# Sparse attention into a capacity-routed expert layer: scaling factors carried beside the rows and applied after the gather, an earlier second search, and a rearranged start

## The chip, the cores and the metric

One Trainium2 chip, one core. The metric is the time of one execution on the device in microseconds (us), the median of several runs. All times below come from the runs and the trace of the kernel before the change.

## The reference

Eight batches of eight heads, sequence 576, head dimension 64, all in fp32. Attention keeps only scores within tau of the row's largest. Its output x has 4608 rows (tokens) of 512 columns, eight blocks of 64, one for each head. A greedy router gives each token to one of eight experts with 576 places each, in order of the logits, and each expert runs a two-layer network on its own rows.

```python
scores = scale * np.matmul(q, k.transpose(0, 1, 3, 2))
thresh = np.max(scores, axis=-1, keepdims=True) - tau
attn = np.exp(masked scores - max);  attn /= attn.sum(-1) + 1e-09
x = (attn @ v) with heads side by side            # [4608, 512]
logits = x @ w_gate                               # [4608, 8]
for idx in np.argsort(-logits.flatten()):         # greedy
    tok, e = idx // 8, idx % 8
    if assigned[tok] >= 0 or counts[e] >= 576: continue
    assigned[tok] = e; counts[e] += 1
for e in range(8):
    out[assigned == e] = np.maximum(x[assigned == e] @ w1[e], 0) @ w2[e]   # 512 -> 1024 -> 512
```

## The kernel before

**Order.** The instructions of every engine stand in the order in which the Python code emits them; an engine takes its own in that order and waits by semaphores for what others make. [...] The names in the rows: PE is TensorE (its weight loads are PEld), DVE VectorE, ACT ScalarE, POOL GpSimd, SP SyncE.

**Attention** (`attention()`, to about 490 us). The 64 heads form 32 pairs; a pair has nine query tiles, so there are 288 tiles, worked two to a slot. For each tile: scores on PE (`sc`), a maximum on DVE (`z`, L74), exponentials on ACT (L85), masking on DVE (L89), transposes on PE (L98) that ACT copies out (`pt`, L113), then products with the values (`pv_unit` L144, `pl_unit` L149) into PSUM banks `xo`, copied to `xt`. The product is not yet divided by the row's denominator. `rd_calc` and `rd_unit` make the reciprocals `rd` and `rm`; `lg_unit`, `lgt_unit`, `lgm_unit` turn `xt` into logits `Lg`. For the last pair these follow each other with nothing beside them.

**Rows to memory** (`xt_unit`). One unit transposes 128 tokens of a batch back to token-major (L201) and stores them to `xrows` [4608, 512] in DRAM. The eight blocks of a row are multiplied by the eight reciprocals there. For the first two batches DVE does this as it empties the bank. The 30 units of the other six batches are put off ("late") and run beside the router's first search: ACT copies the bank (L214, 24 units) and POOL multiplies (L214 again, 128x512); six small units of 64 tokens are scaled by ACT in eight pieces (L212).

**Search** (`Router`). For each expert a threshold is searched that leaves 576 tokens. A search is `prep`, then seven steps of a DVE comparison (`cmp`), PE counting (L403), a DVE copy (`cn`), PE (L409), a DVE flag (`jka`), PE (L419 or L424) and new levels on DVE (`E`); then pick, rank and pack, which end in `idx`, the token numbers. `close` takes the chosen tokens out of the logits. Nothing else can start before the first `idx` at 536.60 us but the late units.

**Expert layer** (`moe()`). Round r works on one expert. `rows` issues five gathers by indirect DMA from POOL's queue (L615; four tiles of 128 rows and one, tile 4, of 64), transposes each tile on PE (`pt`, L625), copies it by ACT to the high part `xh` (L628), and DVE subtracts for the low part `xl`. `w1_load` and `w2_load` split the weights likewise: ACT makes `w1h` (L587) and `w2h` (L603), DVE the low parts. Layer one (L1, L645) has 192 matrix products a round (eight blocks of twelve, for two halves of the rows), from which ACT and DVE make `H`; layer two (L2, L665) has 112, five tiles in the order 0, 4, 1, 2, 3. ACT empties a tile to `y` (L668); POOL's queue stores it by an indirect DMA (L672), and POOL joins the two halves of tile 4 (L675) after tile 2. The next round's search runs inside these products, step by step, and the next round's gathers and transposes inside L2.

**The planner.** At the end of `moe()` a small loop emits the products of `ffn` one by one and advances a planned clock with each; jobs (search, loads, rows) wait in a list with planned times and are emitted when the clock passes them. `GA` is the planned time from the gathers to the first transpose, `RW` the pause behind each tile, `LATS` a pause after DVE work in the search. L1 of a round is emitted only after the planner has marked its rows done. So these numbers set where in PE's, ACT's and POOL's order a step stands, not when it runs.

Of the kernel before, what the change touches and what calls it, by code (L numbers as in the profile page):

```python
# [19 lines left out]
PPB=8; LTB=1; VTB=5; HOLD=1; CAPV=3.3; RATE=(2.4,2.4); NBO=2; XAC=(4,); NDEF=4; XTB=4; XTY=1.05; XT0=2.0; XRB=2  # L20


def attention(ctx, tc, qk, vl, tau, wgd, xrows, xts, Lg, nb_batches, ident, swap, R, after_first):
# [14 lines left out]
    def load(p):  # L38
        b,j=divmod(p,4)
        x=ld.tile([128,QK],F32,name="qk"); v=ld.tile([128,5,128],F32,name="vt",bufs=VTB)  # L40
        cut=(0,HS+S,2*(HS+S),QK) if p==0 else (0,QK)
        for n,(c,e) in enumerate(zip(cut,cut[1:])):
            nc.sync.dma_start(x[:,c:e], qk[b,j,:,c:e])
            if p==0 and n==0:
                nc.sync.dma_start(taub, bass.AP(tensor=tau.tensor,offset=tau.offset,ap=[[0,128],[1,1]]))
        if p==0: nc.sync.dma_start(wg,wgd)
        nc.sync.dma_start(v, vl[b,j])
        t={"v":v}; c=0
        for n,w in ((("k",0),HS),(("q",0),S),(("k",1),HS),(("q",1),S),(("ke",1),HS)):
            t[n]=x[:,c:c+w]; c+=w  # L50
        t["ke",0]=t["k",0]
        LD[p]=t
# [92 lines left out]
    def pl_unit(p,f):  # L145
        b,j=divmod(p,4)
        q=slice(f*HS,(f+1)*HS); xo=XO.pop((p,f))
        for h in range(2):
            T.matmul(xo[64*h:64*h+64,:HS],LD[p]["v"][:,4,64*h:64*h+64],PL[p][:,q],start=False,stop=True,skip_group_check=True)  # L149
        if f==1: have[p,"pv"]=1  # L150
        return VB[id(xo)],lambda: A.activation(XT[b][:,j,q],xo[:,:HS],AF.Copy)  # L151

# [5 lines left out]
    def rd_unit(b):  # L158
        rd=RD[b]
        ps=bank_v([128,512])  # L160
        T.matmul(ps[:,:4],swap,rd[:,:,8],start=True,stop=True)
        rm=wk.tile([128,4,2],F32,name="rm",bufs=XTB+NBO); RD["m",b]=rm
        def ev():
            V.tensor_copy(rm[0:64,:,0],rd[0:64,:,8]); V.tensor_copy(rm[64:128,:,1],rd[64:128,:,8])
            V.tensor_copy(rm[0:64,:,1],ps[0:64,:4]); V.tensor_copy(rm[64:128,:,0],ps[64:128,:4])
        return ev
    LT={}
    def lg_unit(b,f):
        if f==0: LT[b]=wk.tile([128,S+D],F32,name="lt",bufs=LTB)
        ps=bank_v([128,512])  # L170
        for j in range(4):
            T.matmul(ps[32*j:32*j+32,:HS],wg[:,j],XT[b][:,j,f*HS:(f+1)*HS],start=True,stop=True,tile_position=(0,32*j))
        def ev():
            A.activation(LT[b][:,f*HS:(f+1)*HS],ps[:,:HS],AF.Copy)
            if f==1: G.tensor_scalar(LT[b][:,S:],LT[b][:,S-D:S],1.0,0.0,op0=ALU.mult,op1=ALU.add)
        return ev
    def lgt_unit(b):
        ps=bank_v([128,4,128])
        for c in range(4): T.transpose(ps[:,c],LT[b][:,c*128:(c+1)*128],ident)
        def ev():  # L180
            w=wk.tile([128,4,2,4,8],F32,name="lw",bufs=1)
            lv=ps.rearrange("p c (j r) -> p c j r",j=4)
            for h in range(2):
                V.tensor_tensor(w[:,:,h],lv[:,:,:,8*h:8*h+8],RD[b][:,:,h:8:2].rearrange("p j c -> p c j").unsqueeze(3).to_broadcast([128,4,4,8]),op=ALU.mult)
            V.tensor_reduce(Lg[:,4*b:4*b+4,:],w.rearrange("p c h j e -> p c e (h j)"),axis=AX.X,op=ALU.add)
        return ev
    def lgm_unit(b):
        ps=bank_v([128,4,128])
        T.transpose(ps[:,0],LT[b][:,512:640],ident)
        r=slice(64*(b%2),64*(b%2)+64)  # L190
        def ev():
            w=wk.tile([128,4,2,8],F32,name="lwm",bufs=1)
            lv=ps[:,0].rearrange("p (j r) -> p j r",j=4)[:,:,:16].rearrange("p j (h e) -> p j h e",h=2)
            V.tensor_tensor(w[r],lv[r],RD["m",b][r].unsqueeze(3).to_broadcast([64,4,2,8]),op=ALU.mult)
            V.tensor_reduce(Lg[r,32+b//2,:],w[r].rearrange("p j h e -> p e (j h)"),axis=AX.X,op=ALU.add)
        return ev
    def xt_unit(b,c):
        ps=bank_v([128,4,128])
        n=128 if c<4 else 64
        for j in range(4):  # L200
            T.transpose(ps[:n,j],XT[b][:,j,c*128:c*128+n],ident)  # L201
        if b<nb_batches-NDEF-NBO: xr=wk.tile([128,512],F32,name="xr",bufs=XRB)
        else: xr=wk.tile([128,2,S],F32,name="pp",bufs=PPB)[:,0,:512]
        def ev():
            src=RD[b][:,:,2*c:2*c+2] if c<4 else RD["m",b][0:64]
            src=src.unsqueeze(3).to_broadcast([n,4,2,64])
            xv=xr[:n].rearrange("p (j h d) -> p j h d",j=4,h=2); pv=ps[:n].rearrange("p j (h d) -> p j h d",h=2)
            if b<nb_batches-NDEF-NBO: V.tensor_tensor(xv,pv,src,op=ALU.mult)
            elif c in XAC:
                for j in range(4):  # L210
                    for h in range(2):
                        A.activation(xv[:,j,h],pv[:,j,h],AF.Copy,scale=RD[b][:n,j,2*c+h:2*c+h+1] if c<4 else RD["m",b][0:64,j,h:h+1])  # L212
            else:
                A.activation(xv,pv,AF.Copy); G.tensor_tensor(xv,xv,src,op=ALU.mult)  # L214
            nc.sync.dma_start(xrows[b*S+c*128:b*S+c*128+n,:],xr[:n])
        return ev
# [6 lines left out]
    def push_pair(p):  # L223
        b,j=divmod(p,4)
        def when(n): return lambda: have.get((p,n),1<<30)+HOLD<=st["slot"]
        for f in range(2):
# [30 lines left out]
    load(0);   # L257
    if NP>1: load(1)
    after_first()
    for s_ in range(-2,NT//2+2):  # L260
# [10 lines left out]
        flush()  # L271
        for t in ev_:
# [72 lines left out]
class Router:  # L345
# [154 lines left out]
    def close(s):  # L500
        V=s.V; wk=s.wk; L=s.L

        cl=wk.tile([128,8],F32,name="cl"); V.tensor_scalar(cl,s.k("w8"),s.m,-FMAX/2,op0=ALU.is_equal,op1=ALU.mult)
        V.tensor_tensor(L,L,cl.unsqueeze(1).to_broadcast([128,NC_,8]),op=ALU.add)
        u=wk.tile([128,NC_],F32,name="u"); V.tensor_scalar(u,s.sc,BIGS,-FMAX/2,op0=ALU.is_ge,op1=ALU.mult)
        u2=wk.tile([128,NC_],F32,name="u2"); V.scalar_tensor_tensor(u2,s.sc,BIGS+CAP,u,op0=ALU.is_lt,op1=ALU.mult)
        V.tensor_tensor(L,L,u2.unsqueeze(2).to_broadcast([128,NC_,8]),op=ALU.add)
    def warm(s,n):

        ps=s.ps()  # L510
        for i in range(n): s.T.matmul(ps[:,256:384],s.ones,s.tri,start=True,stop=True)
# [26 lines left out]
    def pack(s,first):  # L538
# [4 lines left out]
        if first: s.warm(WARM[0])  # L543
        yield V.wait()
        held(0.7); s.compact(cps,poh,R)
        if first: s.warm(WARM[1])
# [6 lines left out]
LATS=[0.15,0.05,0.4]+[0.6]*5; FIX=(0.125,0.2)  # L553
GA=[7.0,5.5,7.5,9.0]; HALF=1; WARM=[20,4,50]
W1Y=5.0; L2O=(0,4,1,2,3); L2Z=1; HFB=3; RW=[0.2,0.6,1.0,2.0]; LOWP=(0,1); LPF=7; LOWT=1.4; PREPW=1; WLY=(1.0,1.0)

def moe(ctx,tc,R,start,xrows,w1,w2,out,ident):
# [10 lines left out]
    def w1_load(r,s):  # L568
        while r>0 and ("w1",r-1) not in done: yield 0.5
# [21 lines left out]
        done.add(("w1",r))  # L591
    def w2_load(r,s):
# [6 lines left out]
        while ("w1",r) not in done or (r==0 and ("x",0) not in done) or (r>0 and ("l2",r-1) not in done): yield 0.5  # L599
# [9 lines left out]
    def rows(r,s):  # L609
        while r>0 and ("x",r-1) not in done: yield 0.5  # L610
        order=(4,0,1,2,3) if r<=HALF else range(5)
        for t in order:
            n=128 if t<4 else 64
            x=wk.tile([128,D],F32,name="xg",bufs=5); s["xg",t]=x
            G.indirect_dma_start(out=x[:n],out_offset=None,in_=xrows,in_offset=IOA(ap=s["idx"][:n,t:t+1],axis=0))  # L615
        s["ei2"]=wk.tile([128,1],I32,name="ei2",bufs=2); G.tensor_copy(s["ei2"],s["ei"])
        done.add(("g",r))
        yield GA[min(r,3)]
        while r>0 and ("l1",r-1) not in done: yield 0.5
        s["xh"]=wk.tile([128,4,576],F32R,name="xh"); s["xl"]=wk.tile([128,4,576],F32R,name="xl")  # L620
        for t in order:
            n=128 if t<4 else 64
            ps=pt.tile([128,4,128],F32,name="pt")
            held[0]+=0.5
            for d in range(4): T.transpose(ps[:,d,:n],s["xg",t][:n,d*128:(d+1)*128],ident[:n,:n])  # L625
            if t<4: xv=lambda n: s[n][:,:,128*t+32*(t//2):128*t+32*(t//2)+128]; pv=ps
            else: xv=lambda n: s[n].rearrange("p k (a b) -> p k a b",a=2)[:,:,:,256:288]; pv=ps[:,:,:64].rearrange("p k (a b) -> p k a b",a=2)
            A.activation(xv("xh"),pv,AF.Copy)  # L628
            yield 0.8
            V.tensor_tensor(xv("xl"),pv,xv("xh").bitcast(F32),op=ALU.subtract)  # L630
            done.add(("row",r,t))
            if t==1: done.add(("half",r))
            yield RW[min(r,3)]
        done.add(("x",r))

    def ffn(r,s):
        H=wk.tile([128,8,2*CAP],F32R,name="H")
        for f in range(8):
            ps=pf.tile([128,2,512],F32,name="pf")
            for hs in (((0,),(1,)) if r<=HALF and f==0 else ((0,1),)):  # L640
                if hs==(1,): yield None
                for k in range(4):
                    for j,(w,x) in enumerate((("w1h","xh"),("w1h","xl"),("w1l","xh"))):
                        for h in hs:
                            T.matmul(ps[:,h,:HS],s[w][:,k,f*128:(f+1)*128],s[x][:,k,h*HS:(h+1)*HS],  # L645
                                     start=(k==0 and j==0),stop=(k==3 and j==2))
                        if not (k==3 and j==2): yield 0.125*len(hs)
# [31 lines left out]
    def place():  # L679
        for r in range(8):  # L680
# [17 lines left out]
            if r==0:  # L698
                yield from packing(r,s)
                yield 2.3; R.close(); yield 1.4  # L700
# [61 lines left out]
def build(tc, qk, vl, tau, wgd, cst_d, w1, w2, out, off, nb=8):  # L762
    nc=tc.nc
    with ExitStack() as ctx:
# [3 lines left out]
        xrows=dr.tile([8*S,512],F32,name="xrows")  # L768
# [29 lines left out]
```

## Time and profile before

| what | us |
|---|---|
| median of 3 runs | 1036.67 (1036.25 to 1037.45) |
| the profiled execution | 1035.21 |
| its span in the trace | 1033.4, so 1.8 lie outside the span |
| attention | to about 490 |
| first search and packing | 492.13 to 536.60 |
| first L1 product | 547.87 |
| L1 of rounds 1, 2, 3 begins | 619.18, 681.01, 740.36 |
| share of the span that PE / DVE / ACT / POOL are busy | 94 / 75 / 62 / 31% |

The granted clock of TensorE was 0.982 of full speed over the span. Rows of the timeline give start, duration, engine, line, operation, names, shape and count, and in brackets the idle time before on that engine with what ended it. L-numbers are lines of the kernel before.

### The profile page before, as it was taken

What the parts mean: (1) busy time and instruction counts of PE and PEld (TensorE: products, weight loads), DVE (VectorE), ACT (ScalarE), POOL (GpSimd) and SP (SyncE); (2) the same over time, 40 slices, a digit from 0 to 9 for tenths busy, and PEclk for the clock granted to TensorE, in tenths of its full rate; (3) what the DMA queues carried; (4) which work ended last, traced back from release to release, by engine and by line L of the source; (5) the groups of instructions that cost most, each with busy time, mean ns of one, the idle gap of its engine ahead of it and who ended that gap; (6) DMA issues with size and microseconds to landing.
All of it is one profiled execution on the core that took longest, in us unless ns stands there. A gap on an engine that the chain in (4) does not pass through costs nothing. (4 is left out here: it accounts for less than half of the span.)

```text
span 1033.4 us, 24027 instructions
## 1 busy us (share of the span) xinstructions
PE 975.2 (94%) x9104; PEld 709.5 (69%) x9104; DVE 777.4 (75%) x2085; ACT 640.0 (62%) x1221; POOL 323.1 (31%) x485
## 2 busy tenths in 40 slices
PE   6999999999999999998658899999999999999996
PEld 3555555555555555555547779788897978889895
DVE  6999999999999999996777677757585676744230
ACT  5898888888888888886644335444352534445340
POOL 2333333333333343331653445312204031231201
PEclk9999999999999999999878999999999999999998
DMA  6322133233433222302453251504325052363101
GB/s 224 106 67 96 65 138 127 95 138 113 153 107 107 96 72 100 108 2 93 158 206 122 82 169 48 197 28 131 130 83 168 14 185 75 125 229 127 41 11 41
DMA packets 35715, 113.03 MB, mean 109 GB/s; under 512 B 4368, under 2 KB 4752, under 8 KB 35088
## 3 DMA queue, kind: packets, MB, share of 16 engines
q1 hardware_dynamic: 28496, 89.47, 24.5%
q0 software_dynamic: 5888, 18.88, 5.8%
q10 hardware_dynamic: 1216, 3.15, 0.9%
q8 instruction: 72, 1.18, 0.5%
q14 instruction: 43, 0.35, 0.1%
HBM read 89.19 MB, written 21.23 MB: 107 GB/s over the span
## 5 line engine op out<-in xcount | busy, mean ns | idle before, releaser
L75 POOL TENSOR_SCALAR nb<-nb,taub 128x1 f32<-128x1 f32 x288 | 146.8, 510 | 296.6 <-DVE z L74 256.1
L74 DVE TENSOR_SCALAR_CACHE_REDUCE z<-sc 128x576 f32<-128x576 f32 x288 | 206.0, 752 | 34.0 <-PE sc L69 32.5
L85 ACT ACTIVATE pp<-z,nb 128x576 f32<-128x576 f32 x256 | 187.3, 772 | 34.3 <-DVE z L74 32.8
L89 DVE SCALAR_TENSOR_TENSOR pp<-z,nb,pp 128x576 f32<-128x576 f32 x256 | 199.9, 813 | 0.3
L665 PE MATMUL pf<-w2h,H 128*128 128x512 f32 x576 | 196.1, 402 | 1.1 <-DVE H L341 1.1
L69 PE MATMUL sc<-qk 64*128 64x288 f32 (+1 forms) x1280 | 181.3, 428 | 6.0 <-DMA qk<-qk_dram 5.7
L144 PE MATMUL xo<-pt,vt 128*64 128x288 f32 x1024 | 151.9, 418 | 0.7 <-ACT xt L151 0.7
L113 ACT ACTIVATE pt<-tb 128x512 f32<-128x512 f32 x256 | 140.0, 593 | 13.8 <-PE tb L98 11.7
L98 PEld LDWEIGHTS tb<-ident,pp 64*128 64x128 f32 x2304 | 85.7, 139 | 72.7 <-ACT pt L113 16.8
L665 PE MATMUL pf<-w2l,H 128*128 128x512 f32 x320 | 128.2, 401 | 0.0
L672 POOL DMA_INDIRECT out_dram<-y,idx x40 | 42.0, 1050 | 266.8 <-ACT y L668 170.0
L665 PEld LDWEIGHTS pf<-w2h,H 128*128 128x128 f32 x576 | 106.4, 189 | 19.9 <-DVE H L341 1.5
L98 PE MATMUL tb<-ident,pp 64*128 64x64 f32 x2304 | 108.8, 230 | 11.4 <-ACT pt L113 6.2
L69 PEld LDWEIGHTS sc<-qk 64*128 64x128 f32 (+1 forms) x1280 | 94.3, 179 | 35.9 <-DVE pp L89 9.2
L645 PE MATMUL pf<-xh,w1h 128*128 128x288 f32 x512 | 113.3, 300 | 1.2 <-ACT xh L628 1.2
L645 PE MATMUL pf<-xh,w1l 128*128 128x288 f32 x512 | 113.6, 300 | 0.0
L645 PE MATMUL pf<-xl,w1h 128*128 128x288 f32 x512 | 112.8, 299 | 0.0
L651 ACT ACTIVATE hf<-pf 128x576 f32<-128x576 f32 x64 | 41.7, 652 | 105.0 <-PE pf L645 94.0
L144 PEld LDWEIGHTS xo<-pt,vt 128*64 128x64 f32 x1024 | 62.5, 136 | 63.6 <-issue 26.5
L668 ACT ACTIVATE y<-pf 128x512 f32<-128x512 f32 x40 | 23.9, 598 | 115.9 <-PE pf L665 105.1
L645 PEld LDWEIGHTS pf<-xh,w1h 128*128 128x128 f32 x512 | 82.8, 189 | 3.8 <-ACT xh L628 1.7
L645 PEld LDWEIGHTS pf<-xl,w1h 128*128 128x128 f32 x512 | 82.4, 189 | 0.2 <-DVE xl L341 0.2
(170 smaller groups left out, 1355.5 us busy)
## 6 DMA issues: line engine op xcount, KB each, us to landing
qk<-qk_dram SPq DMA_DIRECT2D x31, 1008.0 KB, 4.9
w2s<-w_dram SPq DMA_DIRECT2D x32, 512.0 KB, 5.9
w1s<-w_dram SPq DMA_DIRECT2D x28, 512.0 KB, 5.8
vt<-vl_dram SPq DMA_DIRECT2D x32, 320.0 KB, 5.4
xrows<-pp SPq DMA_DIRECT2D x24, 256.0 KB, 2.0
xts<-xt SPq DMA_DIRECT2D x2, 1152.0 KB, 5.3
pt<-xts SPq DMA_DIRECT2D x2, 1152.0 KB, 6.8
xrows<-xr SPq DMA_DIRECT2D x8, 256.0 KB, 2.0
```

The costliest lines, as they stand in the source:

```text
L69: T.matmul(sc[o,f,:HS], kd["q",h][r,c], kd[k,h][r,:],start=True,stop=True)
L74: V.tensor_scalar(z,SC.pop(t)[:,:,:HS],-0.125,None,op0=ALU.mult,op1=ALU.min,accum_out=nb[:,0:1])
L75: G.tensor_scalar(nb[:,1:2],nb[:,0:1],taub[:,0:1],None,op0=ALU.add)
L85: A.activation(pview(t),ZB[t].rearrange("p a b -> p (a b)"),AF.Exp,bias=NBI[t][:,0:1],scale=-1.0)
L89: V.scalar_tensor_tensor(pv,ZB.pop(t).rearrange("p a b -> p (a b)"),NBI[t][:,1:2],pv,op0=ALU.is_le,op1=ALU.mult,accum_out=den_of(p)[:,p%4, ...
L98: g=slice(64*r,64*r+64); T.transpose(o[:,r],x[g],ident[g,g])
L113: A.activation(PT[p][:,i%2,:,(i//2)*128:(i//2+1)*128].rearrange("p k (r q) -> p r k q",r=2),tb,AF.Copy)
L144: T.matmul(xo[64*h:64*h+64,:HS],v[:,u,64*h:64*h+64],PT[p][:,h,u,q],start=(u==0),stop=False,skip_group_check=True)
L645: T.matmul(ps[:,h,:HS],s[w][:,k,f*128:(f+1)*128],s[x][:,k,h*HS:(h+1)*HS], start=(k==0 and j==0),stop=(k==3 and j==2))
L651: A.activation(hf,ps[:,:,:HS],AF.Relu)
L665: T.matmul(ps[:,0,:],H[:,f,c:c+128],s[w][:,f],start=(f==0 and j==0),stop=e)
L672: G.indirect_dma_start(out=out,out_offset=IOA(ap=s["idx"][:n,t:t+1],axis=0),in_=y[:n],in_offset=None)
```

## The change

1. **Factors.** A row of `xrows` gets 520 columns: 512 unscaled ones and eight reciprocals. A late unit is now an ACT copy of the bank and an ACT copy of 8 columns; POOL's product is gone. In the first two batches DVE copies and POOL writes the factors. The gathers fetch 520 columns, and the gathered tile is scaled before it is transposed: by ACT in eight pieces of 64 columns each with its own factor (L657), or by one DVE product. Round 0 takes ACT for tile 4 and DVE for four tiles; round 1 ACT for tiles 4, 1 and 3; rounds 2 to 7 ACT for all five, 40 instructions a round.
2. **Early second search.** `close` is cut in two and moved into the first packing, and the second search's `prep` and first comparison stand ahead of the first transposes. The low part of round 0's `w1` is made in column blocks on DVE after that, and L1 of round 0 takes its twelve products in an order that uses it last. `LATS`, `GA` and `RW` get other values.
3. **Last pair.** Its value products of the first half are put between the transposes, the reciprocals' swap stands ahead of the 64-row remainders, and the logits use banks of the scores' pool.
4. **Start.** The first pair's load is cut into smaller pieces on two queues (SP and ACT), the gate weights load after pair 1, and 18 products of 128x128 zeros in bf16 run on PE before the first scores.

```diff
-            xv=xr[:n].rearrange("p (j h d) -> p j h d",j=4,h=2); pv=ps[:n].rearrange("p j (h d) -> p j h d",h=2)
-            if b<nb_batches-NDEF-NBO: V.tensor_tensor(xv,pv,src,op=ALU.mult)
-            elif c in XAC:
-                for j in range(4):
-                    for h in range(2):
-                        A.activation(xv[:,j,h],pv[:,j,h],AF.Copy,scale=RD[b][:n,j,2*c+h:2*c+h+1] if c<4 else RD["m",b][0:64,j,h:h+1])
+            if early:
+                V.tensor_copy(xv,ps[:n]); G.tensor_scalar(fv,src,1.0,0.0,op0=ALU.mult,op1=ALU.add)
             else:
-                A.activation(xv,pv,AF.Copy); G.tensor_tensor(xv,xv,src,op=ALU.mult)
+                A.activation(xv,ps[:n],AF.Copy); A.activation(fv,src,AF.Copy)
...
+        def scale(t):
+            if r>1 or (t in (4,1,3) if r==1 else t==4):
+                x=s["xg",t][:128 if t<4 else 64]
+                for h in range(8):
+                    A.activation(x[:,64*h:64*h+64],x[:,64*h:64*h+64],AF.Copy,scale=x[:,D+h:D+h+1])
+                    if r>1: yield 0.22
+                return
+            n=128 if t<4 else 64
+            v=s["xg",t][:n,:D].rearrange("p (h d) -> p h d",h=8)
+            V.tensor_tensor(v,v,s["xg",t][:n,D:XW].unsqueeze(2).to_broadcast([n,8,64]),op=ALU.mult)
...
+        if r==1: yield from scale(order[0])
+        for i,t in enumerate(order):
+            if r>1: yield from scale(t)
+            turn(t)
+            if r==1 and i<4: yield from scale(order[i+1])
+            yield 0.8
+            low(t)
...
-LATS=[0.15,0.05,0.4]+[0.6]*5; FIX=(0.125,0.2)
-GA=[7.0,5.5,7.5,9.0]; HALF=1; WARM=[20,4,50]
+LATS=[0.15,0.2,0.4]+[0.6]*5; FIX=(0.125,0.2)
+GA=[4.5,6.5,7.0,8.0]; HALF=1; WARM=[20,4,50]
...
+        if p==0:
+            a=HS+128; h=HS+S
+            for q,c,e in ((nc.sync,0,a),(nc.scalar,h,h+a),(nc.sync,a,h),(nc.scalar,h+a,2*h),(nc.sync,2*h,QK)):
+                q.dma_start(x[:,c:e], qk[b,j,:,c:e])
...
+    def idles(n):
+        for i in range(n): T.matmul(ps[:,:128],idle,idle,start=True,stop=True)
+    idles(18)
```

The change moves instructions at the borders between rounds. First POOL's queue in L2 of round 0, before the change (`out_dram<-y` is the store of an output tile, `xg<-xrows` a gather of the next round):

```order
L672 DMA out_dram<-y,idx 4608x512
L615 DMA xg<-xrows,idx 64x512
L615 DMA xg<-xrows,idx 128x512 x4
L616 COPY ei_8893<-e 128x1
L672 DMA out_dram<-y,idx 4608x512 x2
L675 TENSOR_TENSOR y_8916<-y_8916,z_8918 64x512
L672 DMA out_dram<-y_8916,idx 4608x512
```

and the same place after it:

```order
L737 DMA out_dram<-y,idx 4608x512 x3
L740 TENSOR_TENSOR y_8807<-y_8807,z_8809 64x512
L737 DMA out_dram<-y_8807,idx 4608x512
L649 DMA xg<-xrows,idx 64x520
L649 DMA xg<-xrows,idx 128x520 x4
L650 COPY ei_8984<-e 128x1
```

The five gathers of round 1 stood behind the first tile's store; now they stand behind the stores of tiles 0, 1, 2 and 4 and the addition, with only tile 3's store after them.

PE at the same border, before: each transpose of a gathered tile (`pt<-ident,xg`) stands between products of L2 (`pf<-w2h,H`), the last of them with 38 products of L2 still to come.

```order
L665 MATMUL pf<-w2h,H 128x512
L625 MATMUL pt<-ident,xg 128x128 x4
L665 MATMUL pf<-w2h,H 128x512
L665 MATMUL pf<-w2l,H 128x512
L665 MATMUL pf<-w2h,H 128x512 x2
L625 MATMUL pt<-ident,xg 128x128 x4
L665 MATMUL pf<-w2l,H 128x512
```

And after, from the last product of L2 of round 0 to the first of L1 of round 1 (`pf<-xh,w1h`); `rps` rows are steps of a search:

```order
L730 MATMUL pf<-w2h,H 128x512
L674 MATMUL pt<-ident,xg 128x64 x4
...
L425 MATMUL rps<-oh,cmp 128x32
L674 MATMUL pt<-ident,xg 128x128 x8
L431 MATMUL rps<-cn,e_566 32x8 x4
L674 MATMUL pt<-ident,xg 128x128 x8
L711 MATMUL pf<-xh,w1h 128x288
```

All five transposes of round 1's rows now stand between the last product of L2 and the first of L1.

ACT at the next border, in L2 of round 1, before (`y<-pf` empties a tile of L2; the last one is the tile after which L2 is over):

```order
L628 ACTIVATE xh<-pt 128x4x128 x2
L668 ACTIVATE y<-pf 128x512
L628 ACTIVATE xh<-pt 128x8x32
L668 ACTIVATE y<-pf 128x512 x2
L603 ACTIVATE w2h<-w2s 128x512 x2
L651 ACTIVATE hf<-pf 128x576
```

and after:

```order
L657 ACTIVATE xg<-xg 128x64 x5
L733 ACTIVATE y<-pf 128x512
L657 ACTIVATE xg<-xg 128x64
L637 ACTIVATE w2h<-w2s 128x512
L657 ACTIVATE xg<-xg 128x64 x2
L675 ACTIVATE xh<-pt 128x4x128
L657 ACTIVATE xg<-xg 128x64 x3
L637 ACTIVATE w2h<-w2s 128x512
L657 ACTIVATE xg<-xg 128x64 x5
L675 ACTIVATE xh<-pt 128x4x128
L637 ACTIVATE w2h<-w2s 128x512
L657 ACTIVATE xg<-xg 64x64 x8
```

All copies `xh` of the next rows stood ahead of L2's last `y`; now that `y` stands amid the scalings of the third tile, and three tiles' scalings and copies, with parts of `w2h` between them, come after it. On PE the transposes of those three tiles stand behind L2's last product. In L2 of rounds 2 to 5 the same holds for fewer: two tiles' transposes stand behind the last product in round 2, one (tile 4) in rounds 3, 4 and 5, none in round 6.

136 lines of the change are left out of this document (88 added, 48 removed).

## The prediction

> **What bounds the kernel now.** I read the span cut into stages first. Columns: busy time of each engine, then the granted clock of PE, DMA share and rate.
>
> ```profile
> core 0: us, PE busy (x) PEld busy (x) DVE busy (x) ACT busy (x) POOL busy (x), PEclk, DMA share, GB/s
> 492.00:532.00 40.00, 24.04 (x223) 18.93 (x223) 28.10 (x64) 23.58 (x72) 27.60 (x24) 0.78 0.51 178
> 548.00:619.00 71.00, 66.05 (x500) 55.80 (x501) 48.77 (x123) 26.03 (x51) 28.48 (x25) 0.97 0.36 120
> 619.00:1014.00 395.00, 393.01 (x2823) 345.63 (x2822) 240.19 (x601) 171.19 (x336) 89.66 (x88) 1.00 0.31 105
> ```
>
> From 619 on PE is busy 393.01 of 395 us: rounds 1 to 7 have nothing to gain, and whatever holds PE there is added to the time in full. The poor stretch is 492 to 532, the first search, where DVE and PE pass a chain to and fro while POOL is busy 27.60 us. So the change can gain before 548 and lose after 584, where the borders between rounds lie. Both sides have to be priced.
>
> **First search: a gain of 9.5.** The groups of that stretch (count, then busy total, mean ns), then single rows of the timeline where POOL does not multiply:
>
> ```profile
> L214 POOL TENSOR_TENSOR pp<-pp,rd 128x512 f32<-128x512 f32 x24 | 27.6, 1174 | 10.3 <-ACT pp L214 10.2
> L214 ACT ACTIVATE pp<-xo 128x512 f32<-128x512 f32 x24 | 14.2, 598 | 12.7 <-PE xo L201 9.4 <-issue 1.7 <-PE sc L419 0.5
> L212 ACT ACTIVATE pp<-xo,rm 64x64 f32<-64x64 f32 x48 | 10.2, 308 | 2.5 <-POOL pp L214 1.5 <-PE xo L201 0.6 <-PE sc L419 0.5
> L341 DVE TENSOR_TENSOR cmp<-b,E 128x1152 bf16<-128x1152 f32 x4 | 7.6, 1904 | 0.1
> L341 DVE TENSOR_TENSOR cmp<-b,E 128x576 bf16<-128x576 f32 x2 | 2.3, 1152 | 0.1
> L341 DVE TENSOR_SCALAR E<-cst,sm 128x34 f32<-128x34 f32 x2 | 2.1, 1054 | 0.1
> L341 DVE TENSOR_TENSOR oh<-oh,ge 128x288 bf16<-128x288 bf16 x1 | 1.3, 1295 | 0.0
> ```
>
> ```profile
> 545.22 0.46 DVE L341 TENSOR_TENSOR oh<-q,qm 128x288 bf16<-128x288 bf16 x1
> 545.93 1.35 DVE L341 TENSOR_TENSOR cmp<-b,cst 128x1152 bf16<-128x1152 f32 x1
> 660.46 0.76 DVE L341 TENSOR_TENSOR cmp<-b,E 128x576 bf16<-128x576 f32 x1
> 666.01 0.30 DVE L341 TENSOR_SCALAR E<-cst,sm 128x34 f32<-128x34 f32 x1
> ```
>
> The same comparison takes 1.90 beside POOL's products and 1.35 without: 4 x 0.55 = 2.2. The half-wide one 2 x 0.39 = 0.8, `E` 2 x 0.75 = 1.5, `oh` 0.8: 5.3 from quoted rows. Other small DVE steps of the stretch add up to about 8 us; as `E` and `oh` show two thirds lost, half of it, some 4.2, is my estimate for them. Together 9.5, with 5.3 and 13 as ends. ACT takes over 30 copies of 8 columns (at 0.21, below, some 6 us) and loses 48 pieces (10.2), so it stays under the 27 us that the search then has.
>
> **Start: a gain of 2.**
>
> ```profile
> 4.21 1.33 PE L69 MATMUL sc<-qk 64*128 64x288 f32 x4 [4.21 <-DMA qk<-qk_dram]
> 7.08 5.73 PE L69 MATMUL sc<-qk 64*128 64x288 f32 x20 [1.53 <-DMA qk<-qk_dram]
> 531.51 2.29 PE L511 MATMUL rps<-trib,onesb 128*128 128x128 bf16 x20 [0.32 <-DVE scol L341]
> ```
>
> The second head's tile waits for its load until 7.08. The load comes in smaller pieces now, half of them from ACT's queue; the first landed 3.5 us after its issue, so the second's first piece may be there near 4.5 and its rest near 5.4, 1.7 earlier; faster score products add a little. Eighteen idle products cost 18 x 0.115 = 2.1 us by the row of 20, in time that PE waits anyway. Ends 0 (DMA delivers no sooner) and 3.5; I take 2. The Trainium skill's page "TensorE: Matmul & The Clock Gate", Part 1, says that PE reaches full clock only after some 3.4 us of sustained work. By that, 2.1 us of idle products would not be enough by 4.2 and the term would be nearer 1.5; the trace of before can't decide it.
>
> **Last pair: a gain of 1.4.**
>
> ```profile
> 487.73 0.35 DVE L165 COPY rm<-xo 64x4 f32<-64x4 f32 x2 [5.53 <-PE xo L161]
> 488.22 1.18 PE L172 MATMUL xo<-xt,wg 128*32 128x288 f32 x16 [0.53 <-DVE rm L165]
> 481.85 0.46 PE L98 MATMUL tb<-ident,pp 64*128 64x64 f32 x8 [1.18 <-ACT pt L115]
> ```
>
> PE waits 1.18 among the last transposes, which the first half's values fill, and 0.53 for `rm`, which is made earlier: 1.7 at most, 0.5 if a wait for `xt` takes their place; 1.4.
>
> **Early second search: a gain of 1 up to L1, nothing later.** `close` is put into the packing, where DVE waits for PE anyway; the low weights (3.7 us on DVE ahead of the first rows) are cut into blocks. From 0 to 2, I take 1. The second search is not needed sooner: its `idx` now stands further along PE's order than before (89 products into L2 instead of 36), so nothing is gained at round 1.
>
> Gains: 9.5 + 2 + 1.4 + 1 = 13.9.
>
> **Border of rounds 0 and 1: a loss of 10.5.** Rows of before, on POOL, PE and ACT:
>
> ```profile
> 598.21 1.91 POOL L615 DMA_INDIRECT xg<-xrows,idx  x1 [4.54 <-issue]
> 600.42 0.95 POOL L615 DMA_INDIRECT xg<-xrows,idx  x1 [0.30 <-issue]
> 602.13 0.46 PE L625 MATMUL pt<-ident,xg 64*128 64x64 f32 x4 [0.59 <-DMA xg<-xrows,idx]
> 603.90 0.66 PE L625 MATMUL pt<-ident,xg 128*128 128x128 f32 x4 [0.32 <-DMA xg<-xrows,idx]
> 604.32 0.70 PE L665 MATMUL pf<-w2h,H 128*128 128x512 f32 x2
> 604.60 0.60 ACT L628 ACTIVATE xh<-pt 128x512 fp32r<-128x512 f32 x1 [1.58 <-PE pt L625]
> 613.06 0.60 ACT L668 ACTIVATE y<-pf 128x512 f32<-128x512 f32 x1 [2.66 <-PE pf L665]
> 613.93 0.97 POOL L672 DMA_INDIRECT out_dram<-y,idx  x1 [6.95 <-ACT y L668]
> 617.41 0.92 POOL L672 DMA_INDIRECT out_dram<-y,idx  x1 [1.19 <-DMA out_dram<-y,idx]
> 618.95 0.40 PE L665 MATMUL pf<-w2h,H 128*128 128x512 f32 x1
> 619.18 0.29 PE L645 MATMUL pf<-xh,w1h 128*128 128x288 f32 x1
> 494.38 1.69 ACT L212 ACTIVATE pp<-xo,rm 64x64 f32<-64x64 f32 x8
> ```
>
> L2 ended at 619.18; call its end E. Tile 2's `y` began at E - 6.1, and tile 4's store left POOL at 618.33, E - 0.8. Behind it the gathers now start at E - 0.5. The first issue takes 1.91 and its rows are there 2.0 later (602.13 after 600.12): E + 3.4; the others follow 1.25 apart and land 2.5 behind their issue, the last near E + 9. From then on ACT's order rules. Eight scalings take 1.7 (1.69), a transpose to its copy 0.7 (603.90 to 604.60), a copy 0.6. Tile 4: 3.4 + 1.7 + 0.7 + 0.35 = 6.1; tile 0, scaled by DVE, copied by 7.2; tile 1 scaled 8.9; a piece of `w1h`, its copy and another piece 10.8; tile 2's copy 11.4; tile 3 scaled 13.1, transposed 13.5. PE has L1 behind that transpose, so it starts at E + 13.5. Five transposes have left L2 (0.42 each by 603.90 to 604.32, 2.1), and the waits there of 0.59 and 0.32 too: 13.5 - 2.1 - 0.9 = 10.5.
>
> **The later borders: a loss of 26.** One more set of rows gives what follows a last product:
>
> ```profile
> 681.01 0.42 PE L645 MATMUL pf<-xh,w1h 128*128 128x288 f32 x2
> 681.26 0.60 ACT L668 ACTIVATE y<-pf 128x512 f32<-128x512 f32 x1 [5.94 <-PE pf L665]
> 681.75 1.14 ACT L603 ACTIVATE w2h<-w2s 128x512 fp32r<-128x512 f32 x2
> ```
>
> Rounds 1 and 2: behind E come `y` (0.25 + 0.55), one scaling 0.21, a piece of `w2h` 0.57, two scalings, 2.0 in all; transpose and copy to 3.3; three scalings, `w2h`, five scalings 5.6; transpose and copy 6.9; `w2h`, eight scalings 9.1; last transpose and copy, 10.3. Less three transposes: 9.0. In the same way, counting what stands behind the last `y`: 5.1 for rounds 2 and 3 (two tiles), 2.2, 1.7 and 3.1 for the next three (tile 4 and what is left of its scalings). Round 6 has its transposes early and loses nothing. Inside L2 a tile costs ACT 1.7 + 0.7 + 0.6 = 3.0 and 0.55 more where a `y` lies between, while PE reaches the next transpose after 10 to 12 products at 0.23 (618.95 to 619.18) and a transpose, 2.7 to 3.2: waits of 2.35, 1.05, 1.95, 2.5 and 1.95 in the five rounds. Search steps on PE lie between those products too and eat about half: 4.9. Sum 9.0 + 5.1 + 2.2 + 1.7 + 3.1 + 4.9 = 26.
>
> The price of eight scalings is the term that all this hangs on. Ends: 0.55, one pass over 512 columns (L214 on ACT, 598 ns, overlapped), and 8 x 0.308 = 2.5 by the group of L212. I take 1.7, as the pieces stand back to back here as in the row of eight.
>
> **Sum.** 1035.2 (the profiled execution, 1.5 under the median of 1036.7) - 13.9 + 10.5 + 26 = 1057.8; 1058 for the time.
>
> **Rivals.** A difference of 0.2%, 2 us, is about what a measurement of this kernel can tell from none.
> - *Scalings at the low end.* At 0.55 a tile the border of rounds 0 and 1 loses three times 1.15 less, the next some 4, the others 2.5, 1.5, 1.3 and 1.7: 36.5 becomes 22, 1044. For it: the pieces are 64 columns and independent of each other. Against it: 1.69 for eight in a row.
> - *The borders are hidden (faster).* If ACT, idle more than half of the time from 619 on (171.19 of 395 busy), has each tile scaled before PE gets there and the late tiles cost no more than their transposes, only rounds 0 and 1 lose: 1035.2 - 13.9 + 10.5 = 1032. It decides where the later borders together cost less than 3.4. Against it: `y` of the last tile stands ahead of some scalings in ACT's order, so they cannot be early.
> - *PE cools in the gaps.* It stands nearly still for some 13 and 10 us at two borders. In the first search, where it mostly waits, the row above has a clock of 0.78 and not 1.00. If the ten microseconds behind each of the two run at that 0.78, each costs some 2, and with the other three borders 4 to 7 come on top: 1063. The page named above has such a rule, a slow clock after an idle window of about 3.4 us; which borders reach that is open here.
> - *The search isn't shorter*, since PE's transposes of late units or ACT hold it: 9.5 goes, 1067. ACT's 0.598 and 0.21 for each of 30 units, 24 us, speak against it.
>
> **Chances.** Forecast (1050 to 1061) 0.42, low-end scalings 0.17, cooling 0.15, no shorter search 0.06, hidden borders 0.17, within 0.2% by a mixture 0.03. Faster 0.17, same 0.03, slower 0.80. For the range I leave out half of the hidden borders and a little above the highest: 1033 to 1068.
>
> **What would show it.** Right: `cmp` 128x1152 near 1.35 and `idx` near 522 to 525 in the first search; L1 of round 1 starting 13 us behind the last product of L2; waits on PE for `xg` and `xh` at five borders that sum to some 35; eight scalings in 1.7. Wrong: PE busy as before from 619 on, gathers landing before L2 ends, or a tile's scalings in well under 1 us.

## The result: 3.1% slower, and the profile after

| | before | changed |
|---|---|---|
| median (us) | 1036.55 (1036.25 to 1037.45) | 1067.99 (1067.14 to 1071.8) |
| ratio, 95% interval | | 1.0309 (1.0294 to 1.0325) |
| span of the profiled execution | 1033.4 | 1065.5 |

It is slower, as forecast, but by 31 us and not by some 22. The median lies at the very end of the range given, which ends at 1068, and the ratio on the median of 1036.67 gives 1068.7, just beyond it.

The stages of the changed kernel, with the columns of the first fence of the prediction:

```profile
492.00:532.00 40.00, 28.22 (x309) 22.96 (x308) 25.93 (x79) 23.18 (x64) 6.62 (x6) 0.86 0.72 241
548.00:619.00 71.00, 61.44 (x414) 49.69 (x413) 43.40 (x109) 29.61 (x71) 21.60 (x22) 0.88 0.29 95
619.00:1014.00 395.00, 376.31 (x2609) 322.13 (x2608) 231.19 (x587) 213.46 (x548) 87.40 (x86) 0.97 0.31 103
```

PE was busy 393.01 of 395 us from 619 on; now it is 376.31, at a clock of 0.97 and no longer 1.00. ACT has 42 us more to do there. To find where, I took the start of each L1 and L2 from the timeline (first product of each) and compared the lengths:

| stage | before | changed | difference |
|---|---|---|---|
| to L1 of round 0 | 547.87 | 532.75 | -15.1 |
| L1 of round 0 | 36.72 | 33.76 | -3.0 |
| L2 of rounds 0, 1, 2, each with the border behind it | 34.59, 32.90, 32.03 | 45.69, 40.88, 36.54 | +11.1, +8.0, +4.5 |
| L2 of rounds 3, 4, 5 | 32.61, 32.38, 30.79 | 34.98, 34.74, 35.53 | +2.4, +2.4, +4.7 |
| L2 of round 6 | 27.96 | 33.38 | +5.4 |
| L1 of rounds 1, 2, 3 | 28.93, 27.32, 27.63 | 32.01, 29.74, 30.28 | +3.1, +2.4, +2.7 |
| L1 of rounds 4, 5, 6 | 27.74, 28.31, 25.38 | 29.47, 27.96, 27.23 | +1.7, -0.4, +1.9 |

So 18.1 us are won before L2 of round 0 and 49.9 lost behind it; the rest, behind the start of L1 of round 7, is 0.3, together 32.1 in the spans.

**The gains.** DVE's groups in the first search of the changed kernel, and two rows of its start and of the last pair:

```profile
L363 DVE TENSOR_TENSOR cmp<-b,E 128x1152 bf16<-128x1152 f32 x4 | 5.4, 1358 | 0.1
L363 DVE TENSOR_TENSOR cmp<-b,E 128x576 bf16<-128x576 f32 x2 | 1.5, 758 | 0.1
L363 DVE TENSOR_SCALAR E<-cst,sm 128x34 f32<-128x34 f32 x2 | 0.5, 274 | 0.1
```

```profile
4.12 1.99 PE L70 MATMUL sc<-qk 64*128 64x288 f32 x8 [0.25 <-DMA qk<-qk_dram]
489.30 0.22 DVE L363 TENSOR_REDUCE b<-Lg 128x8 f32<-128x64 f32 x1
```

Means of 1904, 1152 and 1054 ns have become 1358, 758 and 274. The search from its first step to `scol` took 39.1 us (492.13 to 531.22) and takes 26.6 (489.30 to 515.90): 12.5 won. The search begins 2.8 us earlier, half of it from the start (DVE's first masking at 10.00 for 11.34) and half from the last pair. The second head's tile no longer waits: its four products follow the first's in one row of eight.

**The border of rounds 0 and 1**, timeline rows of POOL, ACT and PE:

```profile
595.24 0.94 POOL L649 DMA_INDIRECT xg<-xrows,idx  x1 [0.30 <-issue]
595.92 0.39 PE L730 MATMUL pf<-w2h,H 128*128 128x512 f32 x1
598.26 2.02 ACT L657 ACTIVATE xg<-xg 64x64 f32<-64x64 f32 x8 [0.75 <-DMA xg<-xrows,idx]
604.44 2.00 ACT L657 ACTIVATE xg<-xg 128x64 f32<-128x64 f32 x8
605.07 1.91 PE L674 MATMUL pt<-ident,xg 128*128 128x128 f32 x4 [3.08 <-ACT xg L657]
610.01 2.01 ACT L657 ACTIVATE xg<-xg 128x64 f32<-128x64 f32 x8
612.20 0.59 PE L711 MATMUL pf<-xh,w1h 128*128 128x288 f32 x1
```

POOL starts the first gather within a microsecond of L2's last product, at 595.24, and L1 starts 16 us behind that product. Each group of eight scalings is in the way. A tile's four transposes took 0.6 us before; those at 605.07 take 1.9, since they start as their parts are scaled and PE runs slowly (its first product of L1 takes 0.59 us, where 0.29 was usual).

**PE's clock behind the borders.** About the first five microseconds of L1 in rounds 1 to 6, from the full microsecond ahead of each start (last three columns: granted clock, DMA share, GB/s):

```profile
612.00:617.00 5.00, 5.00 (x23) 4.79 (x23) 3.60 (x10) 1.65 (x4) 0.00 (x0) 0.53 0.01 4
685.00:690.00 5.00, 4.91 (x28) 4.76 (x29) 2.51 (x7) 1.08 (x3) 0.00 (x0) 0.67 0.01 3
751.00:756.00 5.00, 4.63 (x26) 4.37 (x27) 2.35 (x5) 1.35 (x3) 0.00 (x0) 0.50 0.09 34
816.00:821.00 5.00, 4.49 (x33) 4.22 (x33) 1.89 (x6) 1.62 (x4) 0.61 (x1) 0.70 0.15 56
880.00:885.00 5.00, 4.43 (x41) 4.13 (x42) 2.59 (x9) 1.99 (x5) 0.98 (x1) 1.00 0.13 52
944.00:949.00 5.00, 4.67 (x23) 4.67 (x24) 1.73 (x3) 1.31 (x3) 2.92 (x3) 0.66 0.25 75
```

If work goes in proportion to the clock, five microseconds at 0.53, 0.67, 0.50, 0.70, 1.00 and 0.66 lose 2.4, 1.7, 2.5, 1.5, 0 and 1.7 us, 9.8 in all. This is an estimate. The L1s are longer by 3.1, 2.4, 2.7, 1.7, -0.4 and 1.9, 11.4. The one round that starts at full clock is the one whose L1 isn't longer.

Run 11 below repeats that border (rounds 4 and 5) with the same instructions and the same 2.1 us from L2's last product to L1. The first five microseconds of L1 of round 5, changed kernel first, then run 11:

```profile
880.84:885.84 5.00, 5.00 (x46) 4.84 (x47) 3.40 (x8) 2.32 (x5) 0.23 (x1) 1.00 0.13 52
878.61:883.61 5.00, 5.00 (x35) 4.78 (x36) 1.96 (x6) 1.50 (x3) 0.21 (x1) 0.66 0.13 52
```

L1 of round 5 took 27.96 us in the first and 29.46 in the second; run 3 has 0.66 and 29.47 there too. So the low clock by itself costs 1.5 us here, near the 1.7 of the estimate, and the same border gives it in one execution and not in another.

### The profile page after: what moved, and what is told of

Its sections match the earlier page's. It is cut to its first block, busy times and chain, and to the rows that moved or that the text cites. A ratio compares the mean times of both kernels' runs of the same rounds, so it can differ in the third digit from the quotient of the medians.

```text
span 1065.5 us, 24325 instructions
## 1 busy us (share of the span) xinstructions
PE 999.2 (94%) x9122; PEld 723.6 (68%) x9122; DVE 768.1 (72%) x2104; ACT 700.8 (66%) x1481; POOL 298.3 (28%) x471
## 5 line engine op out<-in xcount | busy, mean ns | idle before, releaser
L86 ACT ACTIVATE pp<-z,nb 128x576 f32<-128x576 f32 x256 | 187.1, 772 | 32.1 <-DVE z L75 30.7
L114 ACT ACTIVATE pt<-tb 128x512 f32<-128x512 f32 x256 | 140.2, 594 | 13.9 <-PE tb L99 11.4
L145 PEld LDWEIGHTS xo<-pt,vt 128*64 128x64 f32 x1024 | 62.5, 136 | 63.5 <-issue 26.2
L733 ACT ACTIVATE y<-pf 128x512 f32<-128x512 f32 x40 | 23.9, 597 | 111.9 <-PE pf L730 87.9
L711 PEld LDWEIGHTS pf<-xh,w1l 128*128 128x128 f32 x512 | 84.9, 197 | 0.8 <-issue 0.8
```

The costliest lines, as they stand in the source:

```text
L86: A.activation(pview(t),ZB[t].rearrange("p a b -> p (a b)"),AF.Exp,bias=NBI[t][:,0:1],scale=-1.0)
L114: A.activation(PT[p][:,i%2,:,(i//2)*128:(i//2+1)*128].rearrange("p k (r q) -> p r k q",r=2),tb,AF.Copy)
L145: T.matmul(xo[64*h:64*h+64,:HS],v[:,u,64*h:64*h+64],PT[p][:,h,u,q],start=(u==0),stop=False,skip_group_check=True)
```

## The experiments

Theory A: a gathered tile's chain on ACT and PE (scalings, transpose, copy) holds PE where the order leaves it no room, and the pause slows PE. Theory B: one part alone does it, the places in the order or the price of the scalings. Lengths of stages below are from each run's timeline, as in the table above; ratios are to the kernel before on the same chip.

**1. No scalings on ACT in rounds 1 to 7.**

```diff
-                    A.activation(x[:,64*h:64*h+64],x[:,64*h:64*h+64],AF.Copy,scale=x[:,D+h:D+h+1])
+                    if r==0: A.activation(x[:,64*h:64*h+64],x[:,64*h:64*h+64],AF.Copy,scale=x[:,D+h:D+h+1])
```

> The changed kernel without the scalings of gathered rows by ScalarE in rounds 1 to 7 (their output rows are therefore unscaled; two tiles of round 1 keep theirs on DVE); every other instruction stands where it stood. Theory A (eight scalings of 2.0 us in a tile's chain hold PE at the borders, and the pause slows PE's clock): the borders lose most of what they cost from round 2 on, some 20 to 25 us, and L1 behind them comes back to some 27.5 us, so 1035 to 1045. Theory B (the places alone do it: gathers behind stores, transposes behind L2's last product): under 8 us are won, 1060 or more.

This kernel leaves the factors out of most rows, so it only serves to measure. Measured: 1040.79, ratio 1.0033 (1.0023 to 1.0042). 27 us of the loss go with 264 small instructions that stand off PE. L2 of rounds 0 to 6 is 39.5, 35.4, 34.6, 33.5, 33.3, 32.0 and 28.0: rounds 3 to 6 are nearly back, while L2 of round 0 keeps 4.9 and those of rounds 1 and 2 2.5 each. That remainder is the part of the places. The L1s did not all come back to 27.5 as theory A had it: rounds 1 to 3, whose first five microseconds ran at 0.70, 0.54 and 0.66, still took 31.4, 30.3 and 30.5; rounds 4 and 5, at full clock, took 28.0.

**2. Idle products at the borders.**

```diff
             for d in range(4):
+                if r>0 and gap[0]: R.warm(8)
                 T.transpose(ps[:,d,:n],s["xg",t][:n,d*128:(d+1)*128],ident[:n,:n])
```

> The changed kernel with eight idle 128x128 bf16 products ahead of each of the four parts of every transpose that stands between L2 and L1, in rounds 1 to 7. Theory A (L1 of rounds 1 to 6 is 2 to 3 us longer than before because PE's clock drops in the gap): L1 starts at most 2 us later and then runs as before the change, 5 to 11 us won, 1057 to 1063. Theory B (L1 is longer for the search steps that moved into it): no gain, 1068 or more by the idle products' own time.

Measured: 1078.18, ratio 1.0387 (1.037 to 1.0405), so as a whole it went as theory B says; the stages say more. The windows of the first five microseconds of L1, of round 2 above and of round 3 below:

```profile
696.00:701.00 5.00, 5.00 (x24) 4.79 (x25) 2.47 (x7) 0.71 (x2) 0.00 (x0) 0.50 0.02 3
768.00:773.00 5.00, 4.53 (x42) 4.13 (x42) 2.07 (x6) 1.50 (x4) 0.00 (x0) 1.00 0.01 3
```

Where the clock was kept, L1 came back: 28.2, 28.0 and 25.9 in rounds 3, 4 and 6 for 30.3, 29.5 and 27.2, which is 5.0 us. In round 2 it wasn't, and L1 took 31.2. In round 1 it was kept at 1.00 too, but L1 came back only from 32.0 to 30.2, with 28.9 before the change: there 1.3 us have another cause, which may be the search steps of theory B. But I had priced the idle products at full clock. While it is low a group of eight takes 1.0 us, and they stretch the border of rounds 0 and 1 by 7.0 us and the next two by 4.5 and 5.3. So the clock's share is shown for three rounds and in part for a fourth; as a remedy it costs more than it gives.

**3. POOL's products back beside the first search.**

```diff
                 A.activation(xv,ps[:n],AF.Copy); A.activation(fv,src,AF.Copy)
+                if c<4:
+                    x4=xr[:n,:512].rearrange("p (j h d) -> p j h d",j=4,h=2)
+                    G.tensor_tensor(x4,x4,one[:n].unsqueeze(3).to_broadcast([n,4,2,64]),op=ALU.mult)
```

> The changed kernel with a product by ones of 128x512 on POOL put back into each late unit of four tiles (24 as before the change, now behind the copy of the factors; the values stay the same). Theory A (DVE's steps of the first search were slowed by POOL's products): the first search is 8 to 12.5 us longer, its comparisons of 1152 columns back at 1.5 to 2.2 us, 1076 to 1080. Theory B (the search was held by ACT's small scalings or by PE): under 3 us, 1068 to 1071.

Measured: 1079.64, ratio 1.0404 (1.0386 to 1.0421), 11.6 us above the changed kernel. The groups of that stretch:

```profile
L220 POOL TENSOR_TENSOR pp<-pp,one 128x512 f32<-128x512 f32 x24 | 28.1, 1193 | 9.8 <-ACT pp L217 9.7
L367 DVE TENSOR_TENSOR cmp<-b,E 128x1152 bf16<-128x1152 f32 x4 | 7.8, 1958 | 0.1
```

The comparison is back at 1958 ns, the search takes 37.9 us for 26.6 (488.82 to 526.74), L1 of round 0 starts 11.7 us later, and behind it the largest difference of a stage is 1.5 us, in L1 of round 5. The gain of the search is POOL's absence.

**4. The start alone, in the kernel before.** The edit is part 4 of the change.

> The kernel before with the changed start alone (pieces on two queues, late gate weights, 18 idle products). By the traces DVE's steady stretch begins 1.3 us earlier (10.00 for 11.34): 1.0 to 1.6 us won, 1035.1 to 1035.6. Rival: the start is hidden behind later waits, 0.

Measured: 1035.88 for 1037.01, ratio 0.9990 (0.9980 to 0.9999): 1.1 us, near the 1.3 of the trace, at the edge of what can be told. In the one traced execution the first search begins 1.7 us earlier (490.40 for 492.13), but L1 of round 0 only 0.2 (547.67 for 547.87), so the trace does not show the gain arriving.

**5. The old planning numbers.**

```diff
-LATS=[0.15,0.2,0.4] ... GA=[4.5,6.5,7.0,8.0] ... RW=[0.2,0.6,0.2,0.6]
+LATS=[0.15,0.05,0.4] ... GA=[7.0,5.5,7.5,9.0] ... RW=[0.2,0.6,1.0,2.0]
```

> The changed kernel with the three lists of planning numbers as they were before the change (LATS, GA, RW); the scalings and all else as changed. The transposes for round 1 then stand 89 to 104 products into L2 of round 0, those for rounds 3 to 6 in L2 with 15 to 19 products between them, and only round 2's rows keep three transposes behind L2's end. Theory A (a tile's chain of 3.2 us on ACT, waited for where the order leaves it no room): all borders but that of rounds 1 and 2 shrink to 0 to 2 us, 20 to 30 us won, 1036 to 1048. Theory B (ACT's scalings cost PE wherever they stand): under 8 us, 1060 or more.

Measured: 1054.07, ratio 1.0164 (1.0142 to 1.0185): 14 us won, under the 20 to 30 expected. L2 of round 0 fell from 45.7 to 38.1, but L2 of round 1 stayed at 40.5 with three transposes behind its end, and that of round 4 rose from 34.7 to 37.1. Against the expectation, the transposes of tile 4 still stand behind L2's last product in rounds 2 and 4. The numbers alone give about half of what run 6 gives.

**6. The next tile's scalings earlier.**

```diff
-        if r==1: yield from scale(order[0])
+        yield from scale(order[0]); yield 0.3
         for i,t in enumerate(order):
-            if r>1: yield from scale(t)
             turn(t)
-            if r==1 and i<4: yield from scale(order[i+1])
-            yield 0.8
+            if i<4: yield from scale(order[i+1])
+            yield 0.3
```

> The changed kernel with the next tile's scalings emitted ahead of this tile's low part in all rounds, LATS 0.05 for the second search, GA 5.5 and RW 0.6: the same 272 scalings on ACT and the same work, the transposes of rounds 2 to 6 now 45 to 103 products into L2, those of round 1 at its end. Theory A: the tails behind L2 go, what stays is about 0.5 us of waiting a tile where they stand 10 products apart, and 6 to 9 us at the border of rounds 0 and 1: 1030 to 1040. Theory B: under 8 us won, 1060 or more.

(The planner's pause between two scalings is also 0.25 for 0.22. There are 280 scalings in rounds 1 to 7 here and not 264 as in the changed kernel, since two tiles of round 1 moved from DVE to ACT; the 272 that the expectation gives counts round 0's eight and belongs to the changed kernel.)

Measured: 1038.05, ratio 1.0005 (0.9995 to 1.0015). 30 us are gone with 16 more scalings than the changed kernel has. What PE waits for from 566 to 1005 us (total, times, longest), changed kernel first, then this one:

```profile
PE pt L674 <- ACT xg L657: 17.0, 20, 3.1
PE rps L441 <- DVE jka L363: 3.0, 3, 2.0
PE pf L711 <- ACT xh L675: 2.4, 5, 0.5
PE pt L674 <- issue: 1.5, 2, 1.2
```

```profile
PE pt L677 <- ACT xg L660: 4.6, 10, 1.0
PE pf L713 <- DVE xl L363: 2.3, 2, 2.1
```

And the first five microseconds of L1 of rounds 2 and 3 run at full clock:

```profile
674.00:679.00 5.00, 5.00 (x44) 4.77 (x45) 2.95 (x7) 2.57 (x5) 2.14 (x1) 1.00 0.19 60
735.00:740.00 5.00, 5.00 (x47) 4.74 (x46) 2.92 (x7) 2.29 (x4) 1.32 (x1) 1.00 0.25 79
```

The waits for `xg` fall from 17.0 to 4.6 us, and L1 of rounds 2 to 4 is 27.9 for 29.5 to 30.3. L2 of rounds 2 to 5 takes 33.1, 32.5, 32.5 and 31.0, within 1.0 us of before the change, so there the scalings cost PE little. Elsewhere they still do: L1 of round 1 takes 36.0 and L2 of round 6 31.8. Run 1 took the price away and left the places; this run left the price and moved the places, on ACT and on PE at once. Either wins 27 to 30 us. That excludes price alone and place alone: it needs both, a chain of 3.3 us a tile and an order that puts it behind L2.

**7. Two of eight blocks on DVE.** As run 6, with `NA=6` and `GA` 5.0 for 5.5: DVE scales the last two blocks of a tile in one product (128x128, 0.29 us).

> As the run before, with six of a tile's eight blocks on ACT and two on DVE in one product (256 columns less work of ACT a tile would be 0.5 us less). Theory A: a tile's chain shrinks from 3.2 to 2.7 us and the waits with it, but the DVE work moves the search and the transposes later by the planner (round 2 at 75 to 105): 1028 to 1040, within 5 us of the run before. Rival: DVE's extra work holds the search, so 5 us or more above the run before.

(Two blocks are 128 columns, not the 256 of the expectation; its 0.5 us is two pieces of 0.25.) Measured: 1034.59, ratio 0.9979 (0.9967 to 0.9990). PE's waits for `xg` from 700 to 1000 us are 1.2 us; L2 of rounds 2 to 4 is 32.1, as before the change. Most of what is left stands at the border of rounds 0 and 1: L2 and L1 there take 74.2 us for 63.5 before. L2 of round 6 takes 31.1 for 28.0.

**8. All scalings of rounds 1 to 7 on DVE.** One product of 0.69 us a tile, and a tile's scaling stands ahead of the low part of the tile before it.

> The changed kernel with all gathered tiles of rounds 1 to 7 scaled by one DVE product of 0.69 us instead of eight ACT pieces; the planner then puts the searches later and nearly all transposes of rounds 3 to 6 behind L2's last product. Theory A (price and place both count: a chain of 0.7 + 0.7 + 0.6 a tile, but five of them behind L2 in four borders): 6 to 9 us at each border, 1050 to 1070. Theory B (only ACT's price counts): the scalings' price gone, as in the run without scalings, 1035 to 1043.

Measured: 1080.3, ratio 1.0411 (1.0388 to 1.0435), slower than both and above what either theory gave. The planner counts DVE's new work and puts the searches later, and with them the gathers and transposes. What PE waits for from 566 to 1005 us, and two rows of the border of rounds 2 and 3:

```profile
PE pt L674 <- issue: 15.9, 8, 5.8
PE pt L674 <- DVE xg L363: 11.7, 12, 2.7
```

```profile
745.17 0.63 ACT L637 ACTIVATE w2h<-w2s 128x512 fp32r<-128x512 f32 x1 [6.74 <-DMA w2s<-w_dram]
747.82 0.66 PE L674 MATMUL pt<-ident,xg 64*128 64x64 f32 x4 [5.80 <-issue]
```

L2 of rounds 2 to 5 takes 46.6, 41.1, 41.1 and 39.7. That is 14.6, 8.5, 8.7 and 8.9 us more than before the change, at a third of the price per tile: the place weighs more than the price. Three of the four are at the upper end of the 6 to 9 expected. What theory A had left out is the first of them and the L1s. In L2 of round 2 the gathers start with L2's last product (731.05 and 731.00), and ACT then waits 6.74 us for the load of `w2`, with the copies of two tiles behind it in its order. The L1s of rounds 1 to 6 are longer by 13.5 us together; their first five microseconds ran at 0.51 to 0.68 of the clock.

**9 and 10. The second search earlier in PE's order.** `GA` of round 0 set to 9.0, with five blocks of round 1 on DVE (9) or two (10).

> As the run with six blocks on ACT and two on DVE, with GA 9.0 for round 0, which only makes the planner put the second search 13 products earlier into PE's order, and three blocks on ACT, five on DVE for round 1. Transposes of round 1 then all stand inside L2 of round 0 (88 to 107), those of round 2 at 82 to 112. If what was left at the border of rounds 0 and 1 (74.2 us for L2 and L1 there, against 63.5 before the change) came from these places, 6 to 10 us are won: 1024 to 1030. Rival: the second search itself is held by DVE, and PE only waits for its steps instead: within 3 us of the run before, 1032 to 1037.

> The same with six blocks on ACT for round 1 too: three of its transposes stand in L2 (92, 99, 107) and two in L1. Theory of places: 4 to 8 us won against the run with GA 4.5, 1027 to 1031, a little above the run with three blocks. Rival as there: 1032 to 1037.

Measured: 1044.36, ratio 1.0060 (1.0047 to 1.0073), and 1035.34, ratio 0.9977 (0.9967 to 0.9986). Run 9 misses both ranges. Run 10 lies in the rival's range, but not for the rival's reason, and wins nothing against run 7's 0.9979. L2 of round 0 and L1 of round 1 took 66.6 and 67.9 us for the 74.2 of run 7, so the place did what it should at that border. In run 9 the L2s of rounds 1 to 6 lost 1.6 to 3.0 us each, with `cn` waited for 4.2 us and `xg` 4.1 us from 700 to 1000; in run 10 L1 of round 6 took 29.7 for 25.6, with one wait of 2.36 us for `hf`. Why moves of the second search reach so far back in the program I have not found.

**11. The last round's scalings beside L1 of round 6.**

```diff
         yield GA[min(r,3)]
+        if r==7:
+            for t in order: yield from scale(t)
...
-            if r>1: yield from scale(t)
+            if 1<r<7: yield from scale(t)
```

> The changed kernel with the scalings of the last round's rows emitted before the wait for L1 of round 6, so beside L1 and no longer between the transposes at the head of L2 of round 6. Theory A (L2 of round 6 takes 33.4 us for 28.0 before the change since each transpose there waits for its eight scalings): L2 of round 6 back at 28 to 29, 4 to 5.4 us won, 1062.5 to 1064. Theory B (PE waits there for something else, or the scalings hold L1's copies on ACT instead): under 1.5 us won.

Measured: 1061.59, ratio 1.0245 (1.0229 to 1.0260): 6.4 us under the changed kernel's 1067.99, which was taken in other runs. In the timeline L2 of round 6 takes 27.98 us, for 33.38 and for 27.96 before the change: 5.4 us are this part's, and theory A holds there. The remaining 1.0 lies in stages that the edit does not touch, which differ both ways (L2 of round 0 43.8 for 45.7, L1 of round 5 29.5 for 28.0).

**12. All of it together**: six blocks on ACT, `GA` 9.0 and the last round's scalings early.

> The run with GA 9.0 and six blocks on ACT in all rounds, with the last round's scalings moved in the same way. Theory A: L2 of round 6 from 31.1 to 28 to 29, 2 to 3 us won, 1032 to 1033.5 and so 0.4% under the kernel before. Theory B: under 1 us.

Measured: 1032.35 for 1036.75, ratio 0.9954 (0.9941 to 0.9968), 0.5% under the kernel before and 3.3% under the change as it was made. The number is theory A's, its step only in part: L2 of round 6 takes 30.0 and not 28 to 29, 1.1 us less than in run 10.

```profile
548.00:619.00 71.00, 67.14 (x504) 57.42 (x502) 49.80 (x119) 37.65 (x90) 28.39 (x29) 1.00 0.28 96
619.00:1014.00 395.00, 389.80 (x2745) 338.85 (x2744) 240.21 (x621) 206.76 (x503) 86.56 (x85) 1.00 0.31 105
```

ACT has nearly the work of the changed kernel from 619 on (206.76 and 213.46), and PE is at 389.80 of 395 and at full clock again. The first 13.2 us of gain (L1 of round 0 at 534.70) still don't all arrive: L2 of round 0 and L1 of round 1 give back 2.3 (65.8 for 63.5), and from L2 of round 5 to L2 of round 6 another 6.8 are lost (90.9 for 84.1).

## Why the prediction was right or wrong

- **The sign and the mechanism held.** That rounds 1 to 7 have no slack, that gathers behind stores and transposes behind L2 would hold PE, and that this outweighs the gains, stands in the table and in runs 1 and 6. One sign did not come: the waits for `xg` and `xh` were to sum to some 35 us, and the rows above have 17.0 and 2.4. All listed waits come to 23.9 us; the L2s grew by 38.5, and what the rest consists of is not split up here.
- **The gains were too small**: 13.9 forecast, 18.1 measured. Search 12.5 for 9.5: I had taken half of the small DVE steps' time as lost to POOL; the 13 that I had as the upper end was nearly reached. Start 1.3 for 2, last pair 1.5 for 1.4; L1 of round 0 gave 3.0, forecast at 1 together with the packing, which lost 0.2. Part of that 3.0 is luck: runs 1, 2, 3 and 11 have the same order in this stage, and there it took 33.2 to 35.2 us for the 36.7 before.
- **The borders of rounds 0 to 5 were about right in sum**: 36.5 forecast, 33.1 measured. The price of eight scalings was 2.0 and not 1.7: the row I took it from reads PSUM, the new pieces read SBUF and write in place. That this is the reason is not shown. The page "ScalarE: Activation LUTs" of the Trainium skill, What ACT_TABLE_LOAD costs, gives some 280 ns plus 0.83 ns a column for an activation with a pointer operand, less 93 back to back; by that eight pieces of 64 would be about 1.9 as an estimate, and the trace agrees with 2.00 to 2.02. At the border of rounds 0 and 1 the 11.1 us for 10.5 came by luck, since two errors cancel. L1 of round 1 began 16.1 us behind L2's last product, not 13.5: tile 2's product on DVE stood behind a low part of `w1` that waited for ACT, and its copy ended 14.0 us behind L2 instead of 11.4. L2 itself, without the transposes and waits, was 5.0 us shorter, not 3.0. One sum is off as well: the rival with scalings at the low end gives 1043, not 1044.
- **The failed step is "Round 6 has its transposes early and loses nothing".** It lost 5.4 us. I had read the transposes' distance from L2's end, and had priced waits inside L2 for five rounds but not for this one. Each tile's scalings stand just ahead of its own transposes in ACT's order, behind L1's last copies, and PE waits for them; run 11 shows it. Rows of the first tile:

```profile
974.12 1.52 ACT L657 ACTIVATE xg<-xg 128x64 f32<-128x64 f32 x6
974.75 0.33 PE L674 MATMUL pt<-ident,xg 128*128 128x128 f32 x1 [0.67 <-ACT xg L657]
```

- **The other failed step is the sum, which left PE's clock out.** It stood among the rivals, with 4 to 7 us on top and a chance of 0.15; the sum itself gave it nothing. The L1s lost 11.4 us, some 9.8 of it by the granted clock. It fell lower than the 0.78 I had taken, to 0.50 to 0.70, and behind five borders. Forecast and rival added, with round 6, would have come to 1067 to 1070.

As to the rule behind that rival, "TensorE: Matmul & The Clock Gate" in the Trainium skill, Part 1, gives a slow clock after some 3.4 us of idling and, in Part 4, says that transposes don't count as busy in the same way. The trace agrees in kind: the clock fell behind five borders. The border of rounds 4 and 5, with 2.1 us from the start of L2's last product to L1 (878.73 to 880.84), left it at 1.00, and that of rounds 3 and 4, with 2.7 (813.92 to 816.63), lowered it to 0.70. But the 2.1 us of the former left it at 0.66 in runs 3 and 11, so the length of the gap alone does not decide, and the limit itself can't be read here.

## What to carry to other kernels

Work taken off a contended engine and put beside a saturated one was nearly free here only where it had its place ahead of the moment at which it is waited for: some 270 small scalings cost 30 us more or less by their place in the order. Count the pauses with what follows them: a gap on PE was paid twice here, as a wait and as slow products behind it. And when an order is set by planned times, price the longest chain per tile with the durations of the trace, and read the result from the order before looking at the engine's busy share.

## What the runs showed of the hardware that I had not expected

- POOL products of 128x512 slowed DVE's comparisons of 1152 columns by 40% (1904 and 1358 ns) and made steps of 34 columns nearly four times as long (1054 and 274). Put back in run 3, they gave 1958 and 625.
- ACT takes 0.25 us for a piece of 64 columns from SBUF (2.00 for eight) and 0.21 from PSUM (1.69 for eight); the former write in place, and no run varies the source alone.
- PE's idle products at a low clock take 1.0 us for eight of 128x128 and 0.6 at full clock, so filling a gap is dear where the clock has already fallen.
- The same border with the same 2.1 us gap was followed by a granted clock of 1.00 in one execution and 0.66 in two others, with L1 behind it at 27.96, 29.46 and 29.47 us.
